# Weight blocks stored from GpSimd's queue in one run per partition, and a norm's logarithm placed behind four exponentials

## The chip, the cores and the metric

The kernel runs on one NeuronCore of a Trainium2 chip. The core has five engines with a queue each: TensorE (PE; PEld is its weight load), VectorE (DVE), ScalarE (ACT), GpSimd (POOL) and SyncE (SP), which only issues DMAs here. DMAs from any queue run on 16 DMA engines. SBUF is the on-chip memory of 128 partitions, PSUM the accumulator memory of the matmuls. The metric is device time in microseconds, the median of several runs.

## The reference

Attention with normalised queries and keys, then a feed-forward block with a squared ReLU. All inputs are float32 but the two weight matrices, which are float64.

```python
# q, k, v: (8, 12, 448, 64); w_in: (768, 2048); w_out: (2048, 768)
def rmsnorm(x, g):
    return x / np.sqrt(np.mean(x * x, axis=-1, keepdims=True) + 1e-06) * g
q_n, k_n = rmsnorm(q, g_q), rmsnorm(k, g_k)
scores = (1 / np.sqrt(64)) * np.matmul(q_n, k_n.transpose(0, 1, 3, 2))
attn = np.exp(scores - np.max(scores, axis=-1, keepdims=True))
attn = attn / (np.sum(attn, axis=-1, keepdims=True) + 1e-09)
x = np.matmul(attn, v)              # -> (8, 448, 12, 64) -> (3584, 768)
h = np.maximum(x @ w_in, 0.0)
out = (h * h) @ w_out               # (3584, 768)
```

## The kernel before

**Stages.** The work is done in four spans of two batch rows each. A stage of attention alone comes first (`attention_alone`, 12 pairs of heads, up to about 134 us). Each span then has a first product (x @ w_in with the squared ReLU, `first_product`) and a second product (`second_product`), and the attention of the next span is spread over the second product of this one. Both products are two-by-two block products by the scheme of Strassen and Winograd, with seven block products in place of eight; they need seven combinations of each set of four weight blocks, called A11, A12, A22, S1, S2, S3 and S4.

**Weights.** The float64 weights are read once as pairs of 32-bit words, rounded to float32 and combined in `prepare(t)`, and the combinations are stored to two DRAM tensors, `w1s` and `w2s`. All later products load them from there (`load_blocks`, tile `sw`, five buffers). There are 32 pieces n; an odd n completes a set, so there are 16 sets, eight for `w1s` and eight for `w2s`. A set's blocks lie in SBUF (`blocks_of(n)`, eight places of 384 columns, part of tile gC), in two buffers that sets take in turn.

**Ticks.** `prepare(t)` is a generator of four quarters, and `weights(...)` runs so many quarters at each `yield` of the attention and of the first product: some 1.2 at each yield of the attention, 1.76 at each of the first product. For piece t: the first quarter clamps on DVE (L603); the second converts the low word on ACT (L606) and shifts on DVE (L608); the third puts sign and exponent together on DVE (L613), and forms S3 and S4 of piece t - 2 on POOL (L583); the third and fourth also write the rounded halves of piece t - 1, on POOL for the first 13 pieces (L575) and on DVE after that (L579). The fourth takes the absolute value of the next piece's high word on ACT (L589), forms S1 and S2 on POOL (L583), and loads further words (L540, L543). 13 of the 35 ticks fall into the attention stage. The set that ends with piece n is stored by SP at the start of tick n + 3 (L598), and `written[0]` then lets `load_blocks` read it.

**The order of the work.** It is written out by hand (`tc.manual_schedule()`): every engine executes its instructions in the order in which the code issues them, and waits on semaphores for data and buffers. So the place of a line sets what stands behind it in its engine's queue.

**A pair's iteration in `attention_alone`.** It has four parts, with a `yield` after each (and so tick work of the weights between them). (1) scores of chunks 0 and 1 with their exponentials on ACT (`scores`, L793 on PE, L797 on ACT), transposes of the next pair's keys (L768), values of the pair before (L851), a running sum of probabilities on DVE (`add_up`, L810), then `norm(i + 2)`: the squares on ACT (L714), their sums on DVE (L715) and a scale on DVE (L716). (2) Transposes of the next pair's queries (evicted by ACT at L772), then `roots(i + 2)`: a logarithm (L725) and an exponential (L726) on ACT, one Newton step on DVE (L727 to L729) and the queries' product with the result on POOL (L730). (3) Scores of chunks 2 and 3 with four exponentials, the sums for the pair before on PE (`total_of`, L876), values of this pair, and `finish(i - 1)` on DVE (L889 to L900). (4) A further `add_up` and `combine_x` on DVE (L910 to L915). `roots` runs for nine pairs, i = 1 to 9.

Of the kernel before, what the change touches and what calls it, by code (L numbers as in the profile page):

```python
# [10 lines left out]
F32 = mybir.dt.float32  # L11
# [376 lines left out]
def attention_then_ffn_bounded(  # L388
# [35 lines left out]
    nc = tc.nc  # L424
# [4 lines left out]
    P = 128  # L429
# [3 lines left out]
    NFC = DFF // P  # L433
    HALF = DM // 2
    HC = NPAIR // 2
    HF = NFC // 2
# [6 lines left out]
    NAT = 2 * NPAIR  # L443
# [10 lines left out]
    dram = ctx.enter_context(tc.tile_pool(name="dram", bufs=1, space=bass.MemoryType.DRAM))  # L454
# [31 lines left out]
    HW = HC * P  # L486
# [6 lines left out]

    A11, S2, S1, S3, A12, A22, S4 = range(7)
    A21 = 7
    w1s = dram.tile([HF, 7, P, HW], F32, name="w1s")
    w2s = dram.tile([7, HF // 4, P, 4, HW], F32, name="w2s")

    def pairs_of(words):
        both = words.rearrange("p (n two) -> p n two", two=2)  # L500
# [16 lines left out]
    def blocks_of(n):  # L517
        at = n // 2 % BLOCKS * 8 * HW
        return stage[:, at:at + 8 * HW].rearrange("p (k m) -> p k m", k=8)

    def place_of(n, k):

        return 7 * int(n >= NFC) if k == A21 else k + int(n < NFC)
# [27 lines left out]
    def prepare(t):  # L551

        def there(n):
            return 0 <= n < 2 * NFC

        def parts(n):
            low, high = pairs_of(words_of(n))
            return exponents_of(n), exponents_of(n).bitcast(U32), low, high  # L560

        def value(n, half):
            if not there(n):
                return

            to = ((A11, A12), (A21, A22)) if n < NFC else ((A11, A21), (A12, A22))
            places = [place_of(n, k) for k in to[n % 2]]
            part = slice(half * HW, (half + 1) * HW)
            if not doubles:
                nc.gpsimd.tensor_copy(blocks_of(n)[:, places[half]], words_of(n).bitcast(F32)[:, part])  # L570
                return
            _, eu, low, _ = parts(n)
            if n < EARLY // 4:
                dst = blocks_of(n)[:, places[half]]
                nc.gpsimd.tensor_tensor(*[x.bitcast(I32) for x in (dst, low[:, part], eu[:, part])], ALU.add)  # L575
            elif half == 0:
                dst = blocks_of(n)[:, places[0]:places[1] + 1:places[1] - places[0]]
                low, eu = (x.rearrange("p (h m) -> p h m", h=2) for x in (low, eu))
                nc.vector.tensor_tensor(*[x.bitcast(I32) for x in (dst, low, eu)], ALU.add)  # L579

        def total(n, dst, x, y, op):
            if there(n) and n % 2:
                nc.gpsimd.tensor_tensor(*[blocks_of(n)[:, place_of(n, i)] for i in (dst, x, y)], op)  # L583

        def unsigned(n):

            if there(n) and doubles:
                e, _, _, high = parts(n)
                nc.scalar.activation(e, high.bitcast(F32), AF.Abs)  # L589

        if t == 0:
            unsigned(0)
        n = t - 3
        if there(n) and n % 2:
            c = n % NFC // 2
            dst = w1s[c] if n < NFC else w2s[:, c // 4, :, c % 4]
            first = place_of(n, A11)
            nc.sync.dma_start(dst.rearrange("k p m -> p k m"), blocks_of(n)[:, first:first + 7])  # L598
            written[0] = n + 1
        if there(t) and doubles:  # L600
            e, eu, low, high = parts(t)

            nc.vector.tensor_scalar(e, e, 2.0 ** -15, 1.875 * 2.0 ** 16, ALU.max, ALU.min)  # L603
        yield
        if there(t) and doubles:
            nc.scalar.activation(low.bitcast(I32), low, AF.Copy, scale=2.0 ** -29)  # L606
            bits = banks.get("bits", eu)
            nc.vector.tensor_scalar(bits, eu, 3, 0x3FFFFFF8, ALU.logical_shift_left, ALU.bitwise_and)  # L608
        if t < 3:
            load_words(t, t - 1)  # L610
        yield
        if there(t) and doubles:
            nc.vector.scalar_tensor_tensor(eu, high, 0xC0000000, bits, ALU.bitwise_and, ALU.bitwise_or)  # L613
        total(t - 2, S3, A11, A21, ALU.subtract)
        total(t - 2, S4, A12, S2, ALU.subtract)
        value(t - 1, 0)
        yield
        unsigned(t + 1)
        value(t - 1, 1)
        total(t - 1, S1, A21, A22, ALU.add)  # L620
        total(t - 1, S2, S1, A11, ALU.subtract)
        load_words(t, t - 1)
        yield
# [20 lines left out]
    def order_of(span, f):  # L644

        return (A11, A12, S2, S1, S3, A22, S4) if span == f == 0 else range(7)
# [4 lines left out]
    def load_blocks(upto):  # L651

        while len(stream) < min(upto, NSPAN * (N1 + N2)):
            n = len(stream) % (N1 + N2)
            if written[0] < min(2 * (n // 7 + 1) if n < N1 else 2 * NFC, 2 * NFC):
                return
            sw = loads.tile([P, 4, P], F32, tag="sw", name="sw", bufs=5)
            if n < N1:
                sw = sw[:, 0:HC]
                src = w1s[n // 7, order_of(len(stream) // (N1 + N2), n // 7)[n % 7]].rearrange("p (c m) -> p c m", c=HC)  # L660
            else:
                n -= N1
                m, i = uses2[n // (HF // 4)]
                src = w2s[i, n % (HF // 4), :, :, m * P:(m + 1) * P]
            nc.sync.dma_start(sw, src)
            stream.append(sw)

# [50 lines left out]
    def roots(i):  # L718


        raw, sq = (places_of(qk, i, n)[:SP] for n in range(2))
        rstd = rstds[i]
        flat = rstd.rearrange("p s n -> p (s n)")
        y, t = (small.tile([P, 2 * S // 32], F32, tag=tag, name=tag)[:SP, 0:4 * NJ] for tag in ("half", "other"))
        nc.scalar.activation(y, flat, AF.Ln, scale=2.0 ** -63)  # L725
        nc.scalar.activation(y, y, AF.Exp, scale=-0.5, bias=sums["rebias"])  # L726
        nc.vector.scalar_tensor_tensor(t, y, -0.5, flat, ALU.mult, ALU.mult)  # L727
        nc.vector.tensor_tensor(t, t, y, ALU.mult)
        nc.vector.scalar_tensor_tensor(flat, t, 1.5, y, ALU.add, ALU.mult)  # L729
        nc.gpsimd.tensor_tensor(sq[:, 0].rearrange("p (j h d) -> p h j d", j=NJ, h=2),  # L730
                                raw[:, 0].rearrange("p (h j d) -> p h j d", j=NJ, h=2),
                                rstd[:, 0].rearrange("p (h j) -> p h j ()", h=2).to_broadcast([SP, 2, NJ, D]),
                                ALU.mult)
# [135 lines left out]
    def total_of(i):  # L869


        tots[i] = ps_o.tile([P, S], F32, tag="t", name="tot")
        parts = [acc_of(i)] + [probs[i, c] for c in range(added(i), NJ)]
        for n, pr in enumerate(parts):
            for h in range(2):
                nc.tensor.matmul(tots[i][h * D:(h + 1) * D, :], sums["ones"], pr[:, h, :],  # L876
                                 start=(n == 0), stop=(n + 1 == len(parts)))
# [39 lines left out]
    def attention_alone():  # L917


        for i in range(NAT):  # L920
            more = i + 1 < NAT
            if 0 < i < NAT - 3:
                load(i + 3)
            scores(i, 0)
            scores(i, 1)
            if i == 0:

                transpose(1, 1, 1)
                scores(0, 2)
                scores(0, 3)  # L930
                transpose(1, 0, 0)
                add_up(0, 1)
                norm(2)
                load_v(1)
                values(0, (0, 1))
                load(3)
                yield
                continue
            if more:
                transpose(i + 1, 1, 0)  # L940
            values(i - 1, (2, 3))
            add_up(i, 1)
            if i + 2 < NAT:
                norm(i + 2)
            elif not more:
                norm(NAT)
                load(NAT + 2)
            yield
            if more:
                transpose(i + 1, 0, 0)  # L950
            load_v(i + 1)
            if i + 2 < NAT:
                roots(i + 2)
            yield
            scores(i, 2)
            scores(i, 3)
            total_of(i - 1)
            values(i, (0, 1))
            finish(i - 1)
            yield  # L960
            if added(i) == 3:
                add_up(i, 2)
            combine_x(i - 1)
            if NAT <= i + 3 < NAT + 2:
                load(i + 3)
            yield
        values(i, (2, 3))
        total_of(i)
        finish(i)
        combine_x(i)  # L970
# [348 lines left out]
```

## Time and profile before

| what | value |
|---|---|
| time, median of 3 runs | 1362.69 us (1361.15 to 1363.36) |
| profiled execution: time, span | 1362.31 us, 1360.5 us |
| PE busy | 1340.5 us (99%) |
| DVE, ACT, POOL busy | 832.1, 430.0, 566.0 us |
| `w1s` and `w2s` stores | 16 issues by SP, 1344 KB each |
| `sw` loads | 224 of 192 KB from `w1s`, 168 of 256 KB from `w2s` |
| granted TensorE clock | 0.997 |

The profile is of one execution; its span runs from the first to the last recorded instruction, and its device time has 1.8 us around that. A line such as L725 is a line of the kernel before. A wait names the engine and line that came last of what an instruction waited for. In the busy times by stage each entry is the busy us of one engine in that stretch of the span.

### The profile page before, as it was taken

Reading aid. Unit: us, or ns where it says so; the run is one execution under the profiler, and the core shown is the slowest. Engines: PE = TensorE matmul, PEld = TensorE weight load, DVE = VectorE, ACT = ScalarE, POOL = GpSimd, SP = SyncE. Lnnn points to the kernel's source line nnn. Section 1 sums busy time; section 2 is a strip of 40 time slices with the busy share of each in tenths; the row PEclk is TensorE's granted clock in tenths of the full one; section 3 lists DMA queues with packets and bytes.
Section 4 is the critical chain, followed back from the end, with each engine's and each line's share of the span. In section 5 each row is a group of like instructions: output and inputs, shape, how many; then the busy total and the mean of one; then the engine's idle time right before and its main releaser. Section 6 shows DMA issues by size and latency. Waiting matters only on the chain.

```text
span 1360.5 us, 16880 instructions
## 1 busy us (share of the span) xinstructions
PE 1340.5 (99%) x5618; PEld 641.6 (47%) x5618; DVE 832.1 (61%) x1482; ACT 430.0 (32%) x674; POOL 566.0 (42%) x458
## 2 busy tenths in 40 slices
PE   8999999999999999999999999999999999999998
PEld 3333445444444455444444455444444455555554
DVE  6999788599987333467778523557788633332111
ACT  7886466433332011233332111233333211110000
POOL 5667533466563122655565222446566312220000
PEclk9999999999999999999999999999999999999999
DMA  9777999655685333355675433345765443334443
GB/s 240 208 229 198 314 360 327 183 130 111 130 151 129 99 87 88 100 119 118 135 150 115 113 100 87 101 104 118 142 129 110 105 103 87 87 91 107 106 111 71
DMA packets 434084, 190.12 MB, mean 140 GB/s; under 512 B 282948, under 2 KB 430788, under 8 KB 433988
## 3 DMA queue, kind: packets, MB, share of 16 engines
q1 hardware_dynamic: 427364, 180.33, 52.2%
q0 software_dynamic: 4736, 8.40, 2.5%
q8 instruction: 47, 0.77, 0.2%
q10 hardware_dynamic: 1888, 0.23, 0.1%
q14 instruction: 49, 0.40, 0.1%
HBM read 155.72 MB, written 33.16 MB: 139 GB/s over the span
## 4 chain that ended last, share of the span: by engine, by line
PE 90%; DVE 5%; ACT 3%; DMA 1%; issue 1%; SPq 0%; POOL 0%; ACTq 0%; DVEq 0%
PE ps L1134 37%; PE pd L1068 10%; PE pa L1068 10%; PE pc L1068 10%; PE sc L785 7%; PE pav L862 7%; PE pb L1068 5%; ACT gT L797 1%; DVE gT L810 1%; DVE rstd L715 1%; PE sc L793 1%; DVE gC L613 1%; PE tot L876 1%; DMA gT<-in_moe_w_in_dram 1%; PE pav L851 1%
## 5 line engine op out<-in xcount | busy, mean ns | idle before, releaser
L1134 PE MATMUL ps<-gT,sw 128*128 128x448 f32 x752 | 293.0, 543 | 0.0
L1134 PE MATMUL ps<-gC,sw 128*128 128x448 f32 x576 | 225.2, 543 | 0.0
L1044 POOL TENSOR_TENSOR gT<-gT 128x448 f32<-128x448 f32 x96 | 93.9, 980 | 283.3 <-ACT gT L1040 283.3
L1134 PEld LDWEIGHTS ps<-gT,sw 128*128 128x128 f32 x752 | 141.1, 190 | 146.4 <-issue 142.0
L750 POOL TENSOR_TENSOR half<-half,mhalf 128x28 f32<-128x28 f32 x36 | 175.2, 4868 | 72.7 <-DVE half L749 69.2
L1134 PEld LDWEIGHTS ps<-gC,sw 128*128 128x128 f32 x576 | 108.1, 190 | 112.9 <-issue 110.7
L1068 PE MATMUL pa<-xT,sw 128*128 128x448 f32 x384 | 155.0, 540 | 0.6 <-ACT p L1072 0.6
L1040 ACT ACTIVATE gT<-gT 128x448 f32<-128x448 f32 x96 | 55.3, 577 | 311.2 <-DVE gT L1083 311.2
L787 ACT ACTIVATE pr<-sc 128x896 f32<-128x896 f32 x87 | 77.5, 915 | 121.7 <-PE sc L785 121.7
L785 PE MATMUL sc<-qkT 64*64 64x448 f32 (+1 forms) x1152 | 109.8, 496 | 0.0
L1068 PEld LDWEIGHTS pa<-xT,sw 128*128 128x128 f32 x384 | 72.9, 190 | 72.6 <-issue 70.7
L583 POOL TENSOR_TENSOR gC<-gC 128x384 f32<-128x384 f32 x64 | 76.2, 1209 | 62.2 <-DVE gC L579 60.4
L1083 DVE TENSOR_TENSOR gT<-z,pd 128x448 f32<-128x448 f32 x32 | 19.8, 620 | 97.8 <-PE pd L1068 97.6
L1068 PE MATMUL pd<-xT,sw 128*128 128x448 f32 x192 | 77.9, 542 | 1.3 <-DVE z L1075 1.3
L1068 PE MATMUL pd<-xC,sw 128*128 128x448 f32 x192 | 77.5, 540 | 1.3 <-DVE gT L1083 1.3
L1068 PE MATMUL pb<-xC,sw 128*128 128x448 f32 x192 | 77.5, 540 | 0.1
L752 POOL TENSOR_TENSOR qk<-qk,half 128x448 f32<-128x448 f32 x72 | 76.4, 1081 | 2.8
L1068 PE MATMUL pc<-xC,sw 128*128 128x448 f32 x192 | 77.4, 539 | 0.0
L1068 PE MATMUL pc<-xT,sw 128*128 128x448 f32 x192 | 77.4, 539 | 0.0
L830 POOL DMA_DIRECT2D xT<-factors x72 | 38.0, 532 | 94.7 <-DMA factors<-square 63.9
L862 PE MATMUL pav<-pr,vt 64*64 64x448 f32 x348 | 72.7, 537 | 0.0
L862 PE MATMUL rest<-pr,vt 64*64 64x448 f32 x348 | 72.7, 537 | 0.0
(144 smaller groups left out, 1849.6 us busy)
## 6 DMA issues: line engine op xcount, KB each, us to landing
sw<-w1s SPq DMA_DIRECT2D x224, 192.0 KB, 2.4
sw<-w2s SPq DMA_DIRECT2D x168, 256.0 KB, 3.2
w1s<-gC SPq DMA_DIRECT2D x8, 1344.0 KB, 6.4
w2s<-gC SPq DMA_DIRECT2D x8, 1344.0 KB, 6.1
out_dram<-osb SPq DMA_DIRECT2D x186, 56.0 KB, 1.9
qk<-in_q_dram SPq DMA_DIRECT2D x144, 56.0 KB, 3.5
qk<-in_k_dram SPq DMA_DIRECT2D x144, 56.0 KB, 3.0
xT<-factors POOLq DMA_DIRECT2D x72, 112.0 KB, 3.4
```

Source lines behind the costliest of these rows:

```text
L583: nc.gpsimd.tensor_tensor(*[blocks_of(n)[:, place_of(n, i)] for i in (dst, x, y)], op)
L750: nc.gpsimd.tensor_tensor(half, half, mhalf, ALU.pow)
L752: nc.gpsimd.tensor_tensor(qkn[:, s], raw[:, s], half[:, s * NG:(s + 1) * NG].rearrange("p g -> p g ()").to_broadcast([P, NG, 32]), ALU.mult)
L785: nc.tensor.matmul(sc[part, h, 0:n], qkT[rows, 0, 1, keys], qkT[rows, 0, 0, of], start=True, stop=True)
L787: nc.scalar.activation(pr, sc[:, :, 0:n], AF.Exp)
L830: nc.gpsimd.dma_start(xT[h * D:(h + 1) * D, b % 2, hp], sums["out"][i % 2].rearrange("(h g) t -> h () (g t)", h=2)[h].to_broadcast([D, S]))
L862: nc.tensor.matmul(into, vs[i][rows, h, c, :], probs[i, c][rows, h, :], start=(c == 0), stop=(c == NF), skip_group_check=True)
L1040: nc.scalar.activation(g, src, AF.Relu)
L1044: nc.gpsimd.tensor_tensor(g, g, g, ALU.mult)
L1068: nc.tensor.matmul(ps, stream[n + at][:, c], rhs[:, c], start=first and c == 0, stop=c == HC - 1, skip_group_check=not first)
L1083: add(g, x, ps, ALU.add)
L1134: nc.tensor.matmul(ps, stream[n][:, c % 4], rhs_of[i][:, c], start=c == 0, stop=c == HF - 1)
```

## The change

The store of a set moves from SP, at the start of tick n + 3, to POOL, in the third quarter of tick n + 2, behind the instruction that forms S4. `written` is raised at the same point of the program as before. The DRAM tensors get another order of dimensions, so that a set's seven blocks lie side by side for each partition: the store writes one run of 10752 bytes per partition in place of seven of 1536. The loads of `sw` keep their runs (1536 bytes from `w1s`, 512 from `w2s`), at other distances. And `roots(i + 2)` moves from the second part of a pair's iteration into the third, behind `scores(i, 2)` and `scores(i, 3)`.

```diff
-    w1s = dram.tile([HF, 7, P, HW], F32, name="w1s")
-    w2s = dram.tile([7, HF // 4, P, 4, HW], F32, name="w2s")
+    w1s = dram.tile([HF, P, 7, HW], F32, name="w1s")
+    w2s = dram.tile([HF // 4, P, 4, 7, HW], F32, name="w2s")
...
-        n = t - 3
-        if there(n) and n % 2:
-            c = n % NFC // 2
-            dst = w1s[c] if n < NFC else w2s[:, c // 4, :, c % 4]
-            first = place_of(n, A11)
-            nc.sync.dma_start(dst.rearrange("k p m -> p k m"), blocks_of(n)[:, first:first + 7])
-            written[0] = n + 1
+        if there(t - 3) and (t - 3) % 2:
+            written[0] = t - 2
...
         total(t - 2, S3, A11, A21, ALU.subtract)
         total(t - 2, S4, A12, S2, ALU.subtract)
+        n = t - 2
+        if there(n) and n % 2:
+            c = n % NFC // 2
+            dst = w1s[c] if n < NFC else w2s[c // 4, :, c % 4]
+            first = place_of(n, A11)
+            nc.gpsimd.dma_start(dst, blocks_of(n)[:, first:first + 7])
         value(t - 1, 0)
...
-                src = w1s[n // 7, order_of(len(stream) // (N1 + N2), n // 7)[n % 7]].rearrange("p (c m) -> p c m", c=HC)
+                i = order_of(len(stream) // (N1 + N2), n // 7)[n % 7]
+                src = w1s[n // 7, :, i].rearrange("p (c m) -> p c m", c=HC)
...
-                src = w2s[i, n % (HF // 4), :, :, m * P:(m + 1) * P]
+                src = w2s[n % (HF // 4), :, :, i, m * P:(m + 1) * P]
...
             load_v(i + 1)
-            if i + 2 < NAT:
-                roots(i + 2)
             yield
             scores(i, 2)
             scores(i, 3)
+            if i + 2 < NAT:
+                roots(i + 2)
             total_of(i - 1)
```

## The prediction

> **What bounds the kernel now.** I read the page's busy times first, then busy time by stage, then the waits, then the instructions of one pair in order of time.
>
> The page: TensorE (PE) is busy for all but 20 us of the span, so nothing that only relieves another engine can bring more than those 20 us.
>
> ```profile
> PE 1340.5 (99%) x5618; PEld 641.6 (47%) x5618; DVE 832.1 (61%) x1482; ACT 430.0 (32%) x674; POOL 566.0 (42%) x458
> ```
>
> By stage (length, then busy us of PE, weight load, DVE, ACT, POOL, granted clock, DMA share, GB/s):
>
> ```profile
> 28.00:58.00 30.00, 30.00 (x156) 11.38 (x152) 28.33 (x43) 23.79 (x43) 15.99 (x13) 1.00 0.73 196
> 58.00:116.00 58.00, 53.80 (x276) 20.27 (x275) 55.50 (x80) 47.81 (x87) 40.75 (x32) 1.00 0.80 228
> 116.00:134.00 18.00, 18.00 (x93) 6.54 (x93) 17.45 (x28) 10.31 (x17) 12.45 (x7) 1.00 0.81 219
> 148.00:192.00 44.00, 43.01 (x114) 21.22 (x112) 34.24 (x45) 28.03 (x43) 16.85 (x16) 1.00 0.99 363
> 200.00:260.00 60.00, 60.00 (x161) 30.32 (x160) 45.09 (x64) 31.99 (x51) 23.35 (x23) 1.00 0.84 287
> ```
>
> Both parts of the change act before 260 us; from 200 us on PE has no gap. In the attention stage (to 134 us) PE and VectorE (DVE) are both full: PE has no gap from 28 to 58 and from 116 to 134, and 4.2 us in between. DVE misses 1.7, 2.5 and 0.5 us in the three windows, most of it the 0.02 us steps between its 151 instructions. So the stage has two saturated engines, and DVE is the one that is full throughout.
>
> The waits (waiter, who it waited for, total us, times, longest):
>
> ```profile
> ACT half L725 <- DVE rstd L716: 15.3, 9, 2.6
> DVE other L727 <- ACT half L726: 1.6, 7, 0.6
> SPq L598 <- POOL gC L583: 33.3, 13, 8.4
> PEld pc L1068 <- DMA sw<-w1s: 0.2, 1, 0.2
> ```
>
> ScalarE (ACT) stands still 15.3 us at the logarithm, DVE only 1.6 us behind it. SyncE (SP) stands 33.3 us at the stores that are to be moved, but in the whole span PE waits 0.2 us for a block of weights and no engine waits for a weight word longer than 0.2 us: what queues behind those stores comes early enough.
>
> One pair, DVE and then ACT in order of time (start, us, line):
>
> ```profile
> 97.13 1.21 DVE L715 TENSOR_REDUCE rstd<-qk 112x16 f32<-112x1024 f32 x1
> 98.38 0.17 DVE L716 TENSOR_SCALAR rstd<-rstd 112x16 f32<-112x16 f32 x1
> 98.46 0.55 DVE L603 TENSOR_SCALAR gC<-gC 128x768 f32<-128x768 f32 x1
> 99.17 0.17 DVE L727 SCALAR_TENSOR_TENSOR other<-half,rstd 112x16 f32<-112x16 f32 x1 [0.16 <-ACT half L726]
> ```
>
> ```profile
> 95.30 0.69 ACT L772 ACTIVATE qkT<-pt,gains 128x448 f32<-128x448 f32 x1
> 98.58 0.22 ACT L725 ACTIVATE half<-rstd 112x16 f32<-112x16 f32 x1 [2.60 <-DVE rstd L716]
> 98.83 0.31 ACT L726 ACTIVATE half<-half,rebias 112x16 f32<-112x16 f32 x1
> 99.05 0.94 ACT L606 ACTIVATE gT<-gT 128x768 int32<-128x768 uint32 x1
> 99.86 2.17 ACT L797 ACTIVATE gT<-sc,rstd 112x448 f32<-112x448 f32 x4
> ```
>
> The four exponentials (L797) stand behind a logarithm that waits for DVE, although their scores were ready at 96.9; PE then stands 0.97 us at 100.06 for them. But DVE works without a break: it was behind, and that is why ACT waited.
>
> **What the Trainium skill says.** "DMA: Bandwidth & Descriptors", Issuing engines are not separate DMA queues: a DMA issued elsewhere still runs on the same 16 engines, only issue time is saved. No run yet shows the store on another queue; that SP's 33.3 us cost no engine anything agrees. The same page, Two DMAs through the same engine are not ordered: a load of what a store wrote must wait for its completion; here SP waited 1.0 us at L665 for the last w2s store, so that wait exists now and stays. "GPSIMD Engine Reference", Specifications: GpSimd shares its SBUF interfaces with VectorE, against DVE instructions with two SBUF inputs or in a two-port mode. The trace agrees: L810 takes 1.08 us alone and 1.90 beside POOL, L603 0.55 and 1.38.
>
> **Part 1, the stores.** Removed from SP: 16 issues of 0.38 us (6 us) and their waits. Nothing on the path stood behind them, so worth 0. SP's loads of q, k, v and words go out earlier, under the same buffer waits; cover: PE waited 0.2 us for sw. If that cover failed, the next thing late would be sw (five buffers of 2.25 us).
>
> Added to POOL: 16 issues. The nearest rows are 72 issues at L830, 0.53 us each with 64 rows of 1792 B, and four at L359 with 64 rows of 4 B at 0.54 to 0.70. Length doesn't show, rows might: for 128 rows I take 0.8, between 0.53 and 1.06; in all 8.5 to 17 us. Five fall in the attention stage (ticks 3, 5, 7, 9, 11), where POOL idles 17 of 58 us, and 11 in the first product, where it idles 27 of 44. Behind an issue stand conversions (L575), and three times of the five the norm's product L730. L730 ends 4.1 us or more before the transposes that read it, so a delay of 1 us passes. If POOL has to wait for its own S4 to drain, it is for the tail of a 1.2 us instruction, in the same slack. Direct cost: 0. Through the shared interface 5 x 0.8 us might slow DVE by some 0.4 us each, up to 2 us; or not at all, if the issue doesn't touch it, as I assume.
>
> The store starts no later: in the trace S4 ended at 157.55 and SP issued at 157.58. The new one is issued some 0.8 us after that, and lands in 5.2 us by the page's fit (2.0 us + bytes / 436 GB/s, DMA: Bandwidth & Descriptors, Anatomy of one DMA; 1.376 MB; an estimate), while the trace shows 6.3 from SP; I take 6 to 7.5. Its buffer is written again at 169.07, 11.5 us after the issue: 3 us or more are left. The first read of w2s gets its data no later, as the store no longer waits for SP.
>
> Layout: the store's runs grow from 1536 to 10752 B, which can only shorten it. The loads keep their runs (1536 B from w1s, 512 B from w2s) but step 10752 B between them. They land in 2.4 and 3.2 us now and are asked for some 9 us ahead, so even twice the time is hidden: 0, at most a few tenths; a gain isn't possible where PE has no gap.
>
> **Part 2, the logarithm.** For nine pairs (i = 1 to 9) L725 to L730 move behind exponentials of scores 2 and 3, and behind the weight tick of that yield on ACT, DVE and POOL. Let A be the end of the squares (L714) on ACT. Then ACT has one tick activation 0.81, L772 0.57, four exponentials 2.09, logarithm and exponential 0.57: done at A + 4.04. DVE, late against A by a lag g, has L715 and L716 (1.34) and the ticks' instructions d before L727: ready at A + g + 1.34 + d. Its new wait is 2.7 - g - d, or nothing.
>
> From the trace d is 2.0, 1.5, 0.95, 1.5, 0.55, 1.1, 2.1, 1.5 for i = 2 to 9, and g is 0, 0.9, 1.7, 0.5, 2.1, 1.2, 1.8, 1.3. Waits: 0.7, 0.3, 0.05, 0.7, 0.05, 0.4, 0, 0.0; as they stand 2.2 us. But ACT no longer waits at the logarithm, so from i = 5 on it runs ahead and g grows; then those fall out, leaving 1.0. For i = 1 the wait is some 1.6 us, and is hidden: DVE waits 1.93 us there for PE's sums (L889) anyway. Old waits that go: 1.6. Net: -0.6 us, with +0.6 if g doesn't grow.
>
> ACT's 15.3 us and PE's 4.2 us of gaps close, but DVE must still do its 55.5 us of work in 58, so they turn into a wait for DVE later (its last products at 147, PE's 1.31 us gap there). L730 starts 0.5 to 1.5 us later on POOL; SP's load of q into its place waits as much longer, with v and word loads behind it, and q is needed 10 us later. L730 now runs beside L889 to L891, one-input instructions, and no longer beside L613, which took 1.68 for 0.95 at i = 2 and i = 8: up to -1.4 us. POOL's tick work ahead of it moves forward beside L810: as much the other way. I take 0, between -2 and +2.
>
> **Sum.** Profiled execution 1362.3 (span 1360.5 and 1.8 around it), less 0.6: 1361.7. The median shown is 0.4 above that execution, so 1362.0. Own range of this case: 1359.5 to 1364.5.
>
> **The rivals.**
> *DVE waits at L727 (slower).* If ACT comes to the exponentials no earlier and g is about half of what I read (0.6 on the mean), the eight waits are 2.7 - 0.6 - d: 0.1, 0.6, 1.15, 0.6, 1.55, 1.0, 0, 0.6, in all 5.6, less the old 1.6: +4.0 us. With g at zero it is 10.4 - 1.6 = +9. At the half: 1362.7 + 4.0, some 1367. It decides once g + d is below 2.7 in most pairs. For it: DVE has no slack, and waits in order. Against: four of eight pairs have over 2.6 in the trace, and g should grow. Chance 0.28.
>
> *The path is ACT and PE (faster).* If DVE only looks full because POOL's work stretches it, exponentials 2 us earlier let PE close its 4.2 us of gaps in 58 to 116: 1362.7 - 4.2 = 1358.5. For: the chain goes through L797 and L725 in nearly every pair, and DVE loses up to 0.8 us to POOL in L810. Against: the same POOL work remains. Chance 0.22.
>
> *The store doesn't leave the path free*: a late landing stops the writer of the next set. It needs 11 us for 6.3 and is inside the slower chance.
>
> **How the numbers follow.** The likeliest case has 0.50 and gives 1362.0. A measurement of this kernel can tell about 0.2% (2.7 us) from no change. The likeliest case gives 0.46 within that and 0.02 on either side; the slower rival is wholly slower but for 0.01; the faster one gives 0.19 faster and 0.03 the same. Together: faster 0.21, same 0.50, slower 0.29. The range reaches to both rivals: 1358.0 to 1368.5.
>
> **What would show it.** Right: the wait at L725 falls from 15.3 us below 4; the wait at L727 stays below 2.5; the stores are a POOL row of 16 at 0.5 to 1.1 us, landing below 8; SP has no wait for L583; PE's gaps between 58 and 116 shrink, yet the first product's first matmul stays within 1.5 us of 133.9. Wrong: that matmul moves by over 2.7 us; L727 waits 5 us or more; L579 or L575 waits for a DMA; or PE waits for sw after 260 us.

## The result, and the profile after

The change made the kernel slower: 1367.95 us in the median of six runs (1366.16 to 1370.45) against 1363.10 for the kernel before, also in six (1361.15 to 1363.95). The ratio is 1.0038, with a 95% interval of 1.0024 to 1.0052: some 5 us. The profiled execution took 1366.70 us, its span is 1364.8. The forecast was 1362.0 and most likely no difference.

The line numbers shift: what was L598 is now L616 (the store, on POOL), L603 is L598, L608 is L603, L613 is L608, L725 to L730 are L727 to L732, and L810 is L812. The page of the kernel after begins so:

```profile
PE 1340.7 (98%) x5618; PEld 641.1 (47%) x5618; DVE 841.2 (62%) x1482; ACT 430.1 (32%) x674; POOL 571.0 (42%) x474
```

PE has the same work as before. DVE has the same 1482 instructions and 9.1 us more busy time: they take longer. Where, is told by the busy times by stage (columns as in the prediction):

```profile
28.00:58.00 30.00, 29.55 (x156) 11.29 (x152) 29.38 (x36) 24.33 (x43) 21.19 (x17) 1.00 0.77 224
58.00:116.00 58.00, 51.82 (x262) 19.93 (x262) 56.40 (x81) 46.31 (x84) 33.84 (x31) 0.97 0.69 213
116.00:134.00 18.00, 16.87 (x86) 5.91 (x82) 17.63 (x26) 11.16 (x19) 11.58 (x9) 1.00 0.77 214
148.00:192.00 44.00, 41.14 (x109) 20.35 (x108) 34.40 (x43) 24.98 (x39) 18.78 (x20) 1.00 0.98 351
200.00:260.00 60.00, 60.00 (x161) 30.31 (x160) 45.43 (x58) 35.12 (x55) 28.06 (x30) 1.00 0.84 308
```

PE's gaps from 58 to 116 are 6.2 us, where the kernel before has 4.2, and from 148 to 192 2.9 in place of 1.0. From 200 us on PE is full in both. In PE's instructions in order of time (before, then after), the first matmul of the first product comes 3.0 us later:

```profile
133.89 2.52 PE L1068 MATMUL pa<-xT,sw 128*128 128x448 f32 x6
136.88 2.52 PE L1070 MATMUL pa<-xT,sw 128*128 128x448 f32 x6
```

The first of the second product comes at 270.97 us (before: 266.53). So 3.0 us were lost in the attention stage and 1.4 in the first product, which is the difference of the two spans.

One thing has to be taken out before traces are compared. In most traces here PE's granted clock falls to half for 3.4 us at a time, in one to three places before 270 us. Where PE is busy, each is worth 1.7 us of its work. The kernel before has one such stretch, at 21.9 us, and the change one at 85.4 us (the 0.97 above), so in this comparison they cancel. The kernel before:

```profile
20.00:28.00 8.00, 6.36 (x26) 2.64 (x28) 5.76 (x12) 6.68 (x14) 4.02 (x4) 0.79 1.13 313
```

The waits that the forecast spoke of (waiter, for whom, total us, times, longest):

```profile
ACT half L727 <- DVE rstd L718: 12.2, 6, 3.4
DVE other L729 <- ACT half L728: 0.8, 2, 0.7
PE pd L1070 <- DVE gT L1085: 2.7, 1, 2.7
```

DVE doesn't wait for the logarithm. But see DVE (first fence) and POOL (second) in order of time:

```profile
63.14 2.90 DVE L603 TENSOR_SCALAR gC<-gC 128x768 uint32<-128x768 uint32 x1
84.54 3.28 DVE L608 SCALAR_TENSOR_TENSOR gC<-gC 128x768 uint32<-128x768 uint32 x1
148.27 3.20 DVE L608 SCALAR_TENSOR_TENSOR gC<-words,gC 128x768 uint32<-128x768 uint32 x1
```

```profile
62.99 0.60 POOL L616 DMA_DIRECT2D w1s<-gC  x1 [0.30 <-POOL gC L583]
63.61 2.00 POOL L575 TENSOR_TENSOR gC<-words,gC 128x384 int32<-128x384 int32 x2
84.39 0.59 POOL L616 DMA_DIRECT2D w1s<-gC  x1 [0.30 <-POOL gC L583]
85.00 1.99 POOL L575 TENSOR_TENSOR gC<-words,gC 128x384 int32<-128x384 int32 x2
148.00 0.64 POOL L616 DMA_DIRECT2D w1s<-gC  x1 [0.30 <-POOL gC L583]
148.66 1.99 POOL L575 TENSOR_TENSOR gC<-words,gC 128x384 int32<-128x384 int32 x2
```

L603 takes 0.55 us alone and L608 0.95. Here they end 0.4 to 0.8 us after POOL's second conversion: DVE is held until POOL is through. Each of the first six stores has such an instruction behind it (after the first, at 46.69, it is L812 at 49.22), and the last of the three shown makes the 2.7 us gap of PE at pd (before: 1.3). To compare kernels I add up **DVE's stretching** from 20 to 152 us: for every DVE instruction its duration in the order of time, less the shortest of that line and shape, where the difference is over 0.12 us (the shortest between 20 and 270 us; like instructions that the view merges count as one row). It is 20.1 us before and 30.5 after. Instructions stretched by over 1 us: one before (2.28 us), six after (2.93, 2.35, 2.33, 1.30, 1.26 and 2.25 us).

### The profile page after: what moved, and what is told of

It is laid out like the page before. It is cut to its first block, busy times and chain, and to the rows that moved or that the text cites. A ratio compares the mean times of both kernels' runs of the same rounds, so it can differ in the third digit from the quotient of the medians.

```text
span 1364.8 us, 16883 instructions
## 1 busy us (share of the span) xinstructions
PE 1340.7 (98%) x5618; PEld 641.1 (47%) x5618; DVE 841.2 (62%) x1482; ACT 430.1 (32%) x674; POOL 571.0 (42%) x474
## 4 chain that ended last, share of the span: by engine, by line
PE 89%; DVE 7%; ACT 1%; issue 1%; DMA 1%; POOL 0%; SPq 0%; ACTq 0%; POOLq 0%; DVEq 0%
PE ps L1136 37%; PE pd L1070 10%; PE pa L1070 10%; PE pc L1070 10%; PE sc L787 7%; PE pav L864 7%; PE pb L1070 5%; DVE gT L812 2%; DVE gC L608 1%; DVE rstd L717 1%; DVE gC L598 1%; ACT gT L799 1%; DVE gC L603 0%; DMA qk<-in_q_dram 0%; DVE xT L902 0%
```

## The experiments

My first theory (1) was that the issue of a store, 0.3 us of waiting for S4 and 0.6 of issuing, pushes POOL's integer conversions onto DVE's instructions. Rivals were the logarithm's new place (2) and the new layout (3). Each ratio below is to runs of the kernel before that were taken beside it; the first four kernels shared theirs (1363.02 us).

**e1, the stores without the logarithm.** The change, with this undone:

```diff
             load_v(i + 1)
+            if i + 2 < NAT:
+                roots(i + 2)
             yield
             scores(i, 2)
             scores(i, 3)
-            if i + 2 < NAT:
-                roots(i + 2)
```

> The stores and the layout as in the change; the norm's logarithm stays where it was. Theory 1 (an issue on GpSimd, 0.3 us of waiting and 0.6 of issuing, pushes the integer conversions behind it into instructions of VectorE that share the SBUF interface, and those are held until the conversions end): slower than before by 3 to 6 us, at 1366 to 1369, with three or more VectorE instructions stretched by over 1 us before 155 us, each beside a conversion behind a store. Theory 2 (the logarithm's place is what costs, by another order on GpSimd and VectorE): within 1.5 us of before, one stretched instruction as before. Theory 3 (the new layout costs in the loads of sw): slower by 3 to 6 us, but lost after 200 us.

Measured: 1367.34 us, ratio 1.0035 (1.0024 to 1.0046). Stretching 25.3 us, with four instructions over 1 us, all of them beside conversions behind a store. Nearly the whole loss is here. Behind two of the first six stores, at 49.05 and 63.98 us, POOL's conversions and DVE took turns, and nothing was stretched by over 1 us. The first product begins at 134.20 us and the second at 269.74; a stretch at half clock lies between them and none before.

**e2, the logarithm without the stores.** The kernel before, with `roots(i + 2)` moved as in the change.

> The logarithm as in the change; stores on SyncE and the layout as before. Theory 1: within 1.5 us of before, or faster by up to 3, one or two VectorE instructions stretched by over 1 us. Theory 2: slower by 3 to 6 us, 1366 to 1369. Theory 3: within 1.5 us of before.

Measured: 1363.41 us, ratio 1.0005 (0.9996 to 1.0013). No instruction is stretched by over 1 us, all in all 24.5. Theory 2 falls. The first product begins at 131.75 us, 2.1 earlier than before, and the second at 267.14, 0.6 later. But the 2.1 us are hardly the logarithm's: 1.7 of them are the stretch at half clock from 21.9 us, which the kernel before has and e2 has not (its granted clock from 20 to 28 us is 1.00). What e2 lost in the first product is the wait of pd (2.0 us where it was 1.3) and a stretch at half clock behind it: from 146 us, in steps of 3 us, its granted clocks are 0.60 and 0.83, worth 1.7 us again.

**e4, layout and logarithm, the stores from SP.**

```diff
-            nc.gpsimd.dma_start(dst, blocks_of(n)[:, first:first + 7])   # tick n + 2, behind S4
+            nc.sync.dma_start(dst, blocks_of(n)[:, first:first + 7])     # start of tick n + 3
```

> The whole change, but the stores are issued by SyncE where they were before; layout and logarithm as in the change. Theory 1: within 1.5 us of before, or faster by up to 3. Theory 2: 1366 to 1369. Theory 3: 1366 to 1369, with the loss after 200 us and sw landing later than 2.4 and 3.2 us.

Measured: 1364.02 us, ratio 1.0004 (0.9995 to 1.0012), stretching 22.6 us, nothing over 1 us. Theory 3 falls: the layout costs nothing that these runs can tell.

**e3, the stores behind the conversions.** The change, with the store at the end of the tick's last quarter:

```diff
-        n = t - 2                      # third quarter, in front of value(t - 1, 0)
-        if there(n) and n % 2:
...
-            nc.gpsimd.dma_start(dst, blocks_of(n)[:, first:first + 7])
...
         total(t - 1, S2, S1, A11, ALU.subtract)
+        n = t - 2                      # last quarter, behind value(t - 1, 1)
+        if there(n) and n % 2:
...
+            nc.gpsimd.dma_start(dst, blocks_of(n)[:, first:first + 7])
```

> The whole change, but each store is issued by GpSimd at the end of the tick's last quarter, behind both conversions of that tick and not in front of them. Theory 1: the conversions no longer stand behind the issue, so two thirds of the loss goes: within 2 us of before, and the sum of VectorE's stretching before 155 us falls from 30 towards 20 us. Theories 2 and 3: as slow as the change, 1366 to 1369.

Measured: 1366.23 us, ratio 1.0026 (1.0018 to 1.0033), stretching 26.6 us, with two instructions over 1 us. By the medians only a third of the loss went. Theory 1 is not refuted, but the order of conversion and store isn't all of it.

**e5, the same place in the program, from SP.**

```diff
-            nc.gpsimd.dma_start(dst, blocks_of(n)[:, first:first + 7])
+            nc.sync.dma_start(dst, blocks_of(n)[:, first:first + 7])
```

> The whole change, but SyncE issues each store, at the place in the program that the change gives it. Theory 1 (GpSimd's issue shifts its conversions, which hold VectorE): within 1.5 us of before, 1362 to 1364.5, stretching of VectorE before 152 us 22 to 25 us. Rival 4 (what costs is the store's earlier transfer, beside the loads of words, q, k and v): slower by 3 to 5 us.

Measured: 1368.83 us, ratio 1.0044 (1.0031 to 1.0058), against my expectation, and with a stretching of only 21.3 us. This is another loss. The waits of e5, in its first 270 us:

```profile
SPq L616 <- POOL gC L583: 59.6, 14, 9.3
PE pb L1070 <- DMA sw<-w1s: 3.0, 1, 3.0
```

SP reaches the store earlier, stands 59.6 us for S4, and the loads behind it come too late (PE also waits 1.3 us for a load of v). In the change SP has no such wait, so e5 says nothing on the change's own loss. It says that at this place only a queue other than SP's will do.

**e6, the issue without the bulk.** As e4, and a DMA of 2 KB from POOL at the change's place:

```diff
+        n = t - 2
+        if there(n) and n % 2:
+            nc.gpsimd.dma_start(probe[n // 2], blocks_of(n)[:, place_of(n, S4), 0:4])
         value(t - 1, 0)
```

> Stores by SyncE as before, layout and logarithm as in the change, and where the change issues the store GpSimd issues a DMA of 2 KB from S4 into a DRAM tensor that nobody reads, 16 in all: the same wait for S4 and the same issue without the bulk. Theory 1: as slow as the change, 1366 to 1369, stretching before 152 us 26 us or more. Rival 5 (GpSimd's software ring moves the 1.3 MB worse, or takes bandwidth): within 1.5 us of before.

Measured: 1372.41 us, ratio 1.0078 (1.0064 to 1.0092). Stretching 27.6 us, with the change's pattern: 2.33 us at 62.99, 2.32 at 84.36, 1.29 at 102.10, 1.28 at 125.52, 2.24 at 148.07. So neither the bulk nor the store's earlier transfer (rivals 5 and 4 in the expectations) is needed for the holding, the issue is enough. The profiled execution is 6.0 us longer than the change's: PE waits 1.8 us for sw here, and some 3 us are two more stretches at half clock (at 21.6, 106.9 and 151.3 us, where the change has one).

**e7, float conversions.**

```diff
-                nc.gpsimd.tensor_tensor(*[x.bitcast(I32) for x in (dst, low[:, part], eu[:, part])], ALU.add)
+                nc.gpsimd.tensor_tensor(*[x.bitcast(F32) for x in (dst, low[:, part], eu[:, part])], ALU.add)
```

> The whole change, but GpSimd's conversions (L575) add as float32 and not as int32, which leaves out the lowest three bits of the first 13 rounded pieces; same shapes. Theory 1 with the holding put down to the integer form (L583 in float32 lets VectorE in between, a two-input VectorE instruction then takes 1.9 us and not 3 to 4): no VectorE instruction is stretched by over 1.3 us, stretching before 152 us falls from 30 to 26 us or less, and most of the loss goes: 1362.5 to 1365.5. If any conversion holds VectorE: as the change, 1366 to 1369.

Measured: 1369.39 us, ratio 1.0059 (1.0045 to 1.0073), stretching 29.7 us with the same six instructions over 1 us. The integer form is not what holds.

**e8, the two engines alone.** One execution, ten segments; in each, DVE's four instructions begin about when POOL's do.

> All of the computation is left out. VectorE runs four adds of two SBUF inputs (128x896 float32), and then four tensor_scalar on one input, each beside nothing, four integer adds of 128x384 on GpSimd, four float adds, four DMA issues of 1344 KB, and one such issue followed by four integer adds. Theory 1: beside integer adds the first VectorE instruction waits 3 us or more, for all of them; beside float adds each takes up to 0.9 us more; beside DMA issues alone nothing is stretched by over 0.2 us. If the issue itself holds VectorE, the instructions beside DMA issues take 0.5 us or more longer each.

DVE in order of time, the two-input adds beside nothing, integer adds, float adds, four DMA issues, and one issue with four integer adds behind it (start, us for all four):

```profile
8.20 4.43 DVE L58 TENSOR_TENSOR vo<-va,vb 128x896 f32<-128x896 f32 x4
13.85 6.46 DVE L58 TENSOR_TENSOR vo<-va,vb 128x896 f32<-128x896 f32 x4
21.53 6.45 DVE L58 TENSOR_TENSOR vo<-va,vb 128x896 f32<-128x896 f32 x4
29.20 4.43 DVE L58 TENSOR_TENSOR vo<-va,vb 128x896 f32<-128x896 f32 x4
34.84 7.75 DVE L58 TENSOR_TENSOR vo<-va,vb 128x896 f32<-128x896 f32 x4
```

Integer and float adds do the same, and four issues do nothing to DVE, 1.376 MB each. But one issue in front of four adds makes DVE lose 3.3 us in place of 2.0. With one-input instructions it is the same: 2.57 alone and beside issues, 4.58 beside adds, 6.00 beside an issue with adds. This gave a new theory (6): **behind a DMA issue POOL's instructions run on without leaving the shared interface free, until POOL has to wait for something.**

**e9, what stands in front of the adds.** Two engines alone again, in one execution, now with a 4 KB issue.

> All of the computation is left out. VectorE runs four two-input adds (4.43 us alone) beside four float adds on GpSimd that stand behind, in turn: nothing; a DMA issue of 4 KB; the same with eight and eight adds; a memset of 640 columns; a copy of 640 columns; a wait for VectorE; a DMA issue and then a wait for VectorE; and eight and eight adds behind nothing. Theory 6 (behind a DMA issue GpSimd's instructions run on without leaving the shared interface free, until GpSimd waits for something): 6.4 us behind nothing, behind a wait, and behind the issue with a wait; 7.5 us or more behind the issue alone, and 12 or more for eight and eight against 11 without an issue. Rival 7 (whatever stands in front and queues the adds does it): the memset and the copy give 7.5 us too. Rival 8 (the transfer does it, not the issue): 6.4 us behind the small issue.

DVE in order of time: behind nothing, an issue, an issue (8 and 8 adds), a memset, a copy, a wait, an issue and a wait, nothing (8 and 8):

```profile
5.91 6.48 DVE L57 TENSOR_TENSOR vo<-va,vb 128x896 f32<-128x896 f32 x4
13.60 7.90 DVE L57 TENSOR_TENSOR vo<-va,vb 128x896 f32<-128x896 f32 x4
22.72 16.07 DVE L57 TENSOR_TENSOR vo<-va,vb 128x896 f32<-128x896 f32 x8
40.01 6.95 DVE L57 TENSOR_TENSOR vo<-va,vb 128x896 f32<-128x896 f32 x4
48.18 7.05 DVE L57 TENSOR_TENSOR vo<-va,vb 128x896 f32<-128x896 f32 x4
56.63 6.62 DVE L57 TENSOR_TENSOR vo<-va,vb 128x896 f32<-128x896 f32 x4
65.62 6.62 DVE L57 TENSOR_TENSOR vo<-va,vb 128x896 f32<-128x896 f32 x4
74.43 13.65 DVE L57 TENSOR_TENSOR vo<-va,vb 128x896 f32<-128x896 f32 x8
```

POOL's adds in the same segments, first behind nothing, behind the issue, behind the memset, and behind the issue with a wait:

```profile
5.04 6.39 POOL L54 TENSOR_TENSOR po<-pa,pb 128x384 f32<-128x384 f32 x4
13.34 3.83 POOL L54 TENSOR_TENSOR po<-pa,pb 128x384 f32<-128x384 f32 x4
39.62 6.39 POOL L54 TENSOR_TENSOR po<-pa,pb 128x384 f32<-128x384 f32 x4
66.70 6.38 POOL L54 TENSOR_TENSOR po<-pa,pb 128x384 f32<-128x384 f32 x4
```

POOL's column shows it best. Behind anything but an issue its four adds take 6.4 us, because DVE gets its turns. Behind an issue they take 3.83 us, under 1 us each, and DVE gets hardly any; with eight adds as well (16.07 us, against 13.65 behind nothing). A memset or a copy in front changes nothing for POOL (DVE's 6.95 and 7.05 would fit adds that start only 0.4 and 0.3 us ahead of it, and not 0.9), and a wait behind the issue ends it: 6.62 with and without the issue. (What waits there is a copy of one column; in e3 and e10 it is the next instruction of the kernel itself.) Rivals 7 and 8 fall. POOL's lead isn't what matters either: 0.4 us behind the memset (shared) and in e8 behind the issue (held); and in the change DVE's instruction had begun before the conversions, and was held all the same.

Theory 6 also explains e3. Behind four of its first six stores POOL's next instruction waits, and nothing is stretched there; behind the other two a conversion follows without a wait, and these are its two instructions over 1 us (2.36 us at 50.35, 1.16 at 106.54).

**e10, each store in front of a wait.** The change, with the store put aside and issued in front of L732, which waits for DVE:

```diff
-            nc.gpsimd.dma_start(dst, blocks_of(n)[:, first:first + 7])
+            pending.append((dst, blocks_of(n)[:, first:first + 7]))
+            if n >= EARLY // 4:
+                store()                # issues all that is pending
...
         total(t - 1, S2, S1, A11, ALU.subtract)
+        if t >= EARLY // 4 - 1:
+            store()
...
+        store()                        # in roots(), in front of the norm's product
         nc.gpsimd.tensor_tensor(sq[:, 0].rearrange("p (j h d) -> p h j d", j=NJ, h=2),
```

> The whole change, but in the attention stage each store is issued by GpSimd just in front of the norm's product, which waits for VectorE, and the two stores at the seam to the first product at the end of the tick's last quarter; later stores as in the change. Theory 6: the issue is followed by a wait, so no VectorE instruction before 134 us is stretched by over 1.3 us, stretching before 152 us is 25 us or less (change: 30), and the time is 1362 to 1365. If the number of issues alone counts: 1366 to 1369, stretching 28 us or more.

Measured: 1367.62 us, ratio 1.0039 (1.0026 to 1.0053), but the stretching is 21.1 us, close to that of before, with no instruction over 1 us, and the first product begins at 133.17 us (the change: 136.88, with as much half clock). The time is lost behind that, and by my own doing: the set of the seam was stored at 141.72 us, 17 us later than by the change, and so beside the loads, issued from 142.87, for which PE waits:

```profile
PE pd L1079 <- DMA sw<-w1s: 4.1, 1, 4.1
```

From within this gap on the clock is at half for 6.8 us, worth some 3 us more.

**e11, the seam mended.** One line: `if t >= EARLY // 4 - 2:`.

> As e10, but the set of the seam (piece 9), which e10 stored so late that PE waited 4.1 us for its blocks, is stored one tick earlier, behind the tick's conversions, where GpSimd then waits for VectorE. Theory 6: no VectorE instruction before 145 us stretched by over 1.3 us, stretching before 152 us 21 to 25 us, no wait of PE for sw above 0.5 us, and 1361.5 to 1364.5, so the loss of the change is gone with all stores still on GpSimd. If the stores cost otherwise: 1366 or more.

Measured in 21 runs: 1364.66 us, ratio 1.0015 (1.0008 to 1.0022) to 1362.01. PE doesn't wait for sw, the first product begins at 133.72 us and the second at 267.12 (the change: 136.88 and 270.97, of which 1.7 us is half clock that this trace doesn't have). Over half of the loss is gone with all 16 stores on POOL, of which only the first six were moved, to other places among POOL's instructions; the median is 0.2 us above what I expected. The stretching is 26.4 us, more than I expected, with one instruction over 1 us (1.81), and some 2 us of loss stay.

That instruction tells where the 2 us may be. Up to 112 us e10 and e11 are the same code. At the first store of e11 the wait in front of the norm's product was already over when the issue ended: POOL went on after 0.02 us, its conversions took 1.0 us each, and L821 was stretched by 1.81 us. In e10 POOL stood for 0.12 us there, the last conversion took 2.3 us, and the same L821 was stretched by 0.7. Behind it PE has a gap of 1.8 us at 60.4 in e11 that e10 doesn't have, and the first product begins 2.3 us later than in e10 if the clock is taken out. So the place alone may not be enough, and POOL must really stand there; but these are two single traces.

**e12, the logarithm with later ticks.** The kernel e2, with

```diff
-                weights(min(ALL, EARLY + (ALL - EARLY) * (u - 1) // (N1 - 6)))
+                weights(min(ALL, EARLY + (ALL - EARLY) * (u - 3) // (N1 - 8)))
```

> The kernel before with the logarithm as in the change, and the weight ticks of the first product start two of its yields later and end where they did. If the 2.1 us by which the logarithm alone brings the first product forward are lost in the gap in front of pd (2.0 us, behind tick instructions on VectorE) and the slower TensorE clock after it: the gap falls below 0.7 us and the kernel takes 1359.5 to 1362. If they are lost elsewhere: as with the logarithm alone, 1362.5 to 1364.5.

Measured: 1367.05 us, ratio 1.0037 (1.0023 to 1.0051). The wait of pd for L1083 fell to 0.6 us in all, but PE waits 2.4 us for the same line at pb later, and 0.8 for sw, and from the end of the later gap the clock is at half for 3.4 us. The gap moved, it didn't close. The 2.1 us that this run set out to keep were mostly clock (see e2). No version here beats the kernel before.

## Why the prediction was wrong

**The logarithm** cost about what I had worked out, partly by luck. I had 1.0 us of new waits at DVE's Newton step, and it was 0.8; e2 has a ratio of 1.0005. Wrong was that ACT would run ahead and its wait fall below 4 us: it is 12.2 us, and still 8.9 in e2, without the stores. Wrong too was that DVE's sharing with POOL would come to nothing, within 2 us either way: in e2 its stretching is 4.4 us more than before. Only 0.6 us of that shows at the start of the second product.

**The stores' own cost** was right: 0.56 to 0.64 us an issue (I took 0.8, from 0.53 to 1.06), 0.3 us of waiting for S4, 6.8 and 6.9 us to landing in the median (I took 6 to 7.5; single ones up to 8.7), no late buffer, no wait of PE for sw after 260 us, no wait of SP for a store. The new layout cost nothing. That longer runs "can only shorten" the store isn't shown: from SP, in e4 and e2, the median landing is 7.5 and 7.4 us for w1s and 5.6 and 6.2 for w2s.

**The step that failed** is the sentence that through the shared interface the five issues might slow DVE "by some 0.4 us each, up to 2 us; or not at all, if the issue doesn't touch it, as I assume". The issue doesn't touch it (4.43 us beside four issues in e8). What I didn't think of is what the issue does to the instructions behind it. I had named these, conversions and the norm's product, but only asked who waits for them, and not whom they hold. The term that I put at 0 to 2 us measures 6.0 us of stretching against e2, which has everything of the attention stage but the stores (30.5 and 24.5). What came through to PE is best read from when each product begins, with 1.7 us taken off for every stretch at half clock before it (2.8 for the long one of e10, which begins in a gap):

| run | stores | first product, us | second product, us |
|---|---|---|---|
| before | SP | 132.2 | 264.8 |
| e1, old place of the logarithm | POOL, conversions behind | 134.2 | 268.0 |
| e2 | SP | 131.8 | 265.4 |
| e4 | SP, new layout | 131.5 | 265.1 |
| e3 | POOL, two with a conversion behind | 133.2 | 266.2 |
| the change | POOL, conversions behind | 135.2 | 269.3 |
| e7 | the same, float conversions | 136.0 | 269.9 |
| e10 | POOL, in front of waits | 131.5 | 266.5 |
| e11 | POOL, in front of waits | 133.7 | 267.1 |

All rows from e2 on have the logarithm's new place; e5, e6 and e12, which lose time at late loads or moved ticks too, are left out. The stores cost 2.0 us of the attention stage without it (e1 against before) and 3.4 with it (the change against e2), so over half of the 6.0 us goes through in a stage in which DVE has no slack. By the second product it is 3.2 and 3.8 us; a part of that is the gap in front of pd, 2.7 us in both where it is 1.3 before and 2.0 in e2. Each row is one execution, and e10 and e11 show that equal code can differ by 2 us there.

I had also written down what would show me wrong, and it did: the first product's first matmul moved by 3.0 us, over the 2.7 that I allowed, and PE's gaps between 58 and 116 us grew from 4.2 to 6.2.

**The rivals.** The slower one put the loss at DVE's wait for the logarithm; that wait halved instead, from 1.6 to 0.8 us. It had the right engine, and the right reason for which it would hurt, that DVE is full and works in order. The faster one is refuted by e2: with the logarithm moved and the stores left, PE's gaps between 58 and 116 us are 4.2 us, as before.

**What isn't settled.** The runs show that an issue in front makes POOL's adds exclude DVE, and that a wait ends it. It isn't a rule without exceptions: behind two stores of e1 POOL and DVE took turns. Nor is an issue the only thing that does it: the one instruction stretched by over 1 us in the kernel before (L608, 2.28 us at 81.53) is held by conversions with no issue in front of them since POOL's last wait; the first instruction behind that wait is the norm's product, on 112 partitions where the others work on 128. No experiment followed this up. Not shown is why, either. The Trainium skill ("GPSIMD Engine Reference", Instruction dispatch) says that consecutive Pool instructions are no barrier between its eight cores, and (When to use GPSIMD) that two of them write a DMA's descriptors. So the other six might begin the adds while the two still write, and some core would then always be using the interface; a wait would bring them together again. That fits 3.83 us for four adds, but no run here looks at single cores: it is argued, not measured. Whether the hold at the first store is all of the 2 us that e11 keeps is open as well.

## What to carry to other kernels

A DMA moved to GpSimd's queue is not free when its issue is short: ask which GpSimd instructions follow it before GpSimd's next wait, and what VectorE does meanwhile. Put the issue in front of an instruction that waits anyway, if possible one that still waits when the issue is over. And when two engines are both full in a stage, price a change by how long the instructions of each get, not only by the waits between them.

## What was not expected of the hardware

- Behind a DMA issue four GpSimd adds of 128x384 take 3.83 us and hold VectorE, whether the issue moves 1.376 MB or 4 KB, whether the adds are integer or float, and whether VectorE's instructions have one SBUF input or two. Without the issue they share, and take 6.39 us beside two-input instructions and 5.06 beside one-input ones.
- A gap of PE is often paid twice. In the twelve traces of the whole kernel the granted clock falls to half 19 times between 15 and 1340 us, for 3.4 us each (once 6.8), always inside a gap of PE of 1.7 us or more or within 1.7 us of its end; there are 39 such gaps, so about half have one. The same gap can have it in one execution and not in another: e1's gap of 2.7 us in front of pd has it (0.72 in the mean of 6 us behind it), the change's has not. e11's 21 times range over 4.9 us, and the mean clock goes with them: 0.999 in all below 1363.7 us, 0.995 or 0.996 in all above 1365.
